# Part 2 of an attention and two-MoE kernel: four to three places for the split pairs, five to six for the output weights

## The chip, the cores and the metric

One core of a Trainium2 chip runs the whole program in one launch. The metric is the device time of one execution in microseconds; the median of the runs shown is quoted. TensorE (PE) has two clock levels, 1.2 and 2.4 GHz, and the profile gives the granted share of the higher one.

## The reference, cut to what matters

```python
attn = softmax(q @ mean8(k).T / sqrt(64)) @ mean8(v)      # 8 x 8 heads, 576 x 64
x = attn as 4608 tokens x 512
x = max(x @ w1, x @ w2, x @ w3) @ w_out                   # part 1's second half, d_ff 768
h = relu(x @ w_in)                                        # part 2: 512 -> 2048
out = (h * h) @ w_out2                                    # part 2: 2048 -> 512, float32
```

## The kernel before, in words

Part 1 (attention and the first MoE) runs in twelve blocks of 384 tokens and ends near 758 us. Part 2 runs in nine blocks `j` of 512 tokens. All products work on split numbers: a float32 value is written as a high half (ScalarE, L133) and a low half (the difference, VectorE, L134), and each product takes three matmuls (high by high, high by low, low by high). Both matrix products of part 2 are done by a seven-product scheme (Strassen's, in Winograd's form), which is why sums and differences of tiles (`add`, L644, and `minus`, L647) stand between them.

A block has four groups `gr`. Each group has an inner half and an outer half:

- `moe2_in` (L689): seven products with the resident weights `wi2s` (L673, 84 matmuls in all), gathered into the units `c0` to `c3` (one place each) and squared. The products use three PSUM banks `ps`; the first of a group is copied out by ScalarE at L707 into `c0`.
- `moe2_out` (L783): outer products in the order of `OUT`, four in groups 0 and 1, ten in groups 2 and 3 (called light and heavy below; 28 in a block, 252 in all). Each takes a fresh split pair `g` from the pool `g_p` (a pair of [128, 512] halves: 4 KB in each partition), one tile `wo2s` from the pool `wo_p` (also 4 KB), and does 12 matmuls into an accumulator (L797). The first eight of the 12 need only the high half of `g`, the last four need the low half.

The output weights don't stay on chip: `fetch_group` (L806) fetches each of the 252 tiles (512 KB) anew on SP's queue, once for each product. A fetch waits until the product that used its place has ended. Inner weights `wi2s` are fetched once, into `w3_p`, at the change from part 1 to part 2.

The program is not run in the order of the code: a planner with a simulated clock orders each engine's instructions before the launch, with the pools' places among its conditions. In the program before it has put matmuls of the next group's inner half between the outer products of a group; only three of the next group's products fit there, one a bank, until the copy at L707 frees the first. Each engine then runs its own list strictly in order.

At the border between blocks (`j`, group 3) VectorE and ScalarE also mix and split the next block's input: `load_y` (L607) fetches `yr` into places shared with the operands of groups 2 and 3, `mix_y` (L620) and `split_y` (L632) work on it.

Pools on the same side of the on-chip memory lie behind one another: `g_p`, `c_p`, `w3_p`, `wo_p`. With `reuse_waits="tile"` a tile waits only for the older tiles whose bytes it takes over; at the start of part 2 these are tiles of part 1.

Of the kernel before, what the change touches and what calls it, by code (L numbers as in the profile page):

```python
# [86 lines left out]
def leave(pool, size):  # L87

    pool.tile([P, size // 4], F32, name="unused", bufs=1)
# [3 lines left out]
def attention_moe_kernel(ctx: ExitStack, tc: tile.TileContext, q, k, v, vn, w1, w2, w3, wo1, wi2, wo2, out):  # L93
# [561 lines left out]
    add_moe1(NB1 - 1)  # L655
    run()
    s1.close()
    g_p = ctx.enter_context(tc.tile_pool(name="g_p", bufs=4, reuse_waits="tile"))
    c_p = ctx.enter_context(tc.tile_pool(name="c_p", bufs=1, reuse_waits="tile"))
    w3_p = ctx.enter_context(tc.tile_pool(name="w3_p", bufs=1, reuse_waits="tile"))  # L660
    wo_p = ctx.enter_context(tc.tile_pool(name="wo_p", bufs=5, reuse_waits="tile"))
    leave(w3_p, 160)
    leave(wo_p, 32)
    acc_ps = ctx.enter_context(tc.tile_pool(name="acc_ps", bufs=1, space=PSUM, reuse_waits="tile"))
# [208 lines left out]
```

## Time and profile before

| what | before |
|---|---|
| median of 3 runs | 1470.51 us (1463.79 to 1470.95) |
| the profiled execution | 1465.84 us, of it 1464.0 us span |
| PE busy | 1432.9 us, 98% of the span |
| DVE busy | 984.6 us, 67% |
| ACT busy | 763.9 us, 52% |
| DMA moved | 263.94 MB, mean 180 GB/s |
| fetches of output weights | 252 of 512 KB, median 5.7 us from issue to landing |
| chain that ended last | PE 88%, DMA 5%, ACT 3%, DVE 2% |

Times are of one execution on the chip. A bracket behind a row is the engine's idle time before it and what ended that. A matmul's end is modelled: it overlaps the next one, so the distance from one start to the next is less than the duration shown. Weight loads (PEld) overlap in the same way.

### The profile page before, as it was taken

How to read it: one execution, taken by the hardware profiler on the slowest of the kernel's cores; microseconds unless marked ns; L12 is line 12 of the kernel's file. 1: busy time of each engine (PE TensorE's matmuls, PEld its weight loads, DVE VectorE, ACT ScalarE, POOL GpSimd, SP SyncE). 2: the span in 40 equal slices, each digit the busy share in tenths (PEclk: the TensorE clock that was granted, in tenths of full speed). 3: DMA queues.
4: the chain of work that ended last, by engine and by line, in shares of the span. 5: the costliest groups of instructions: out<-in, count | busy, mean ns of one | idle time of the engine just before them, and what ended most of it. 6: DMA issues, size and time to landing. Idle time of an engine off the chain costs nothing.

```text
span 1464.0 us, 27554 instructions
## 1 busy us (share of the span) xinstructions
PE 1432.9 (98%) x10410; PEld 1409.8 (96%) x10410; DVE 984.6 (67%) x1778; ACT 763.9 (52%) x1983; POOL 182.2 (12%) x228
## 2 busy tenths in 40 slices
PE   6989999999999999999999999999999999999998
PEld 4879999999999999999999999999999999999998
DVE  5896466766765856656426768687776768686765
ACT  7794366655665646655314535353444445454443
POOL 3451012222222212222000000000000000000000
PEclk9899999999999999999999999999999999999999
DMA  7553135443355434422539856666666666565746
GB/s 225 185 168 110 53 115 173 141 134 123 120 164 176 126 124 130 130 101 79 187 116 370 290 196 212 220 210 224 229 231 225 227 216 214 198 245 174 274 144 229
DMA packets 118307, 263.94 MB, mean 180 GB/s; under 512 B 12672, under 2 KB 62848, under 8 KB 118176
## 3 DMA queue, kind: packets, MB, share of 16 engines
q1 hardware_dynamic: 111264, 252.75, 51.0%
q10 hardware_dynamic: 6912, 9.44, 1.8%
q8 instruction: 82, 1.34, 0.4%
q14 instruction: 49, 0.40, 0.1%
HBM read 213.91 MB, written 48.23 MB: 179 GB/s over the span
## 4 chain that ended last, share of the span: by engine, by line
PE 88%; DMA 5%; ACT 3%; DVE 2%; issue 1%; POOL 0%; SPq 0%; DVEq 0%; ACTq 0%; POOLq 0%
PE ps L513 28%; PE ps L673 23%; PE ps L532 10%; PE accB L797 6%; PE accA L797 6%; DMA wo2s<-wo_dram 4%; PE accF L797 3%; PE accE L797 3%; PE sc L353 2%; PE accD L797 2%; PE tr L381 2%; PE av L410 1%; PE av L409 1%; ACT ss L358 1%; DVE wbits L165 1%
## 5 line engine op out<-in xcount | busy, mean ns | idle before, releaser
L513 PE MATMUL ps<-x,w 128*128 128x384 f32 x2592 | 495.7, 342 | 3.3 <-ACT w L133 1.2
L513 PEld LDWEIGHTS ps<-x,w 128*128 128x128 f32 x2592 | 452.0, 190 | 6.1 <-ACT w L133 2.6
L673 PE MATMUL ps<-y,wi2s 128*128 128x256 f32 x3024 | 371.8, 277 | 0.5 <-DVE c L644 0.2
L673 PEld LDWEIGHTS ps<-y,wi2s 128*128 128x128 f32 x3024 | 356.6, 188 | 1.9 <-DVE c L644 0.8
L532 PE MATMUL ps<-h,wo 128*128 128x384 f32 x864 | 162.1, 339 | 3.2 <-POOL wo L134 2.4
L532 PEld LDWEIGHTS ps<-h,wo 128*128 128x128 f32 x864 | 149.5, 189 | 4.0 <-POOL wo L134 2.8
L686 ACT ACTIVATE c<-c 128x512 f32<-128x512 f32 x90 | 56.3, 627 | 167.2 <-DVE c L644 166.6
L644 DVE TENSOR_TENSOR c<-ps,c 128x512 f32<-128x512 f32 x144 | 98.2, 687 | 66.0 <-PE ps L673 64.5
L521 DVE TENSOR_TENSOR hm<-ps,hm 128x384 f32<-128x384 f32 x144 | 79.5, 552 | 72.3 <-PE ps L513 69.9
L133 ACT ACTIVATE g<-c 128x512 fp32r<-128x512 f32 x144 | 90.2, 626 | 56.7 <-DVE c L683 23.3
L797 PE MATMUL accA<-wo2s,g 128*128 128x256 f32 x864 | 115.8, 277 | 0.0
L797 PE MATMUL accB<-wo2s,g 128*128 128x256 f32 x864 | 110.9, 277 | 2.6 <-DMA wo2s<-wo_dram 1.9
L134 DVE TENSOR_TENSOR g<-c,g 128x512 fp32r<-128x512 f32 x144 | 97.6, 685 | 16.2 <-ACT g L133 16.2
L797 PEld LDWEIGHTS accA<-wo2s,g 128*128 128x128 f32 x864 | 107.1, 188 | 0.0
L358 ACT ACTIVATE ss<-sc,st 128x72 f32<-128x72 f32 (+1 forms) x320 | 97.9, 319 | 17.6 <-DVE st L355 15.4
L797 PEld LDWEIGHTS accB<-wo2s,g 128*128 128x128 f32 x864 | 103.9, 188 | 3.2 <-ACT o L766 1.6
L364 POOL TENSOR_TENSOR ss<-ss,st 128x432 f32<-128x432 f32 (+1 forms) x64 | 56.4, 882 | 265.7 <-DVE st L363 182.9
L413 DVE TENSOR_TENSOR xf<-av,xf 64x192 f32<-64x192 f32 (+1 forms) x112 | 50.7, 453 | 46.7 <-ACT xf L412 44.8
L385 DVE TENSOR_TENSOR pt<-tr,pt 72x192 fp32r<-72x192 f32 (+1 forms) x112 | 49.3, 449 | 41.4 <-ACT pt L384 40.1
L412 ACT ACTIVATE xf<-av 64x192 f32<-64x192 f32 (+1 forms) x112 | 45.4, 405 | 54.5 <-PE av L410 40.4
L133 ACT ACTIVATE h<-hm 128x384 fp32r<-128x384 f32 x72 | 37.7, 523 | 64.2 <-DVE hm L521 63.9
L358 ACT ACTIVATION_READ_ACCUMULATOR ss<-sc,st 128x1 f32 (+1 forms) x320 | 65.8, 206 | 0.0
(104 smaller groups left out, 1951.4 us busy)
## 6 DMA issues: line engine op xcount, KB each, us to landing
wo2s<-wo_dram SPq DMA_DIRECT2D x252, 512.0 KB, 5.7
wi2s<-wi_dram SPq DMA_DIRECT2D x24, 512.0 KB, 9.1
wraw<-in_wo_dram SPq DMA_DIRECT2D x22, 512.0 KB, 3.7
wraw<-in_w_dram SPq DMA_DIRECT2D x18, 512.0 KB, 3.4
y_dram<-ys ACTq DMA_DIRECT2D x48, 192.0 KB, 2.0
wraw<-in_wi_dram SPq DMA_DIRECT2D x16, 512.0 KB, 3.5
wi_dram<-wraw SPq DMA_DIRECT2D x16, 512.0 KB, 3.7
wo_dram<-wraw SPq DMA_DIRECT2D x64, 128.0 KB, 2.0
```

What stands on the lines that cost most here:

```text
L133: nc.scalar.activation(hi, src, AF.Copy)
L134: engine.tensor_tensor(out=lo, in0=src, in1=as_f32(hi), op=ALU.subtract)
L358: nc.scalar.activation(ss[:, i, h], src[:, i, h], AF.Exp, bias=st[:, 0, i, h : h + 1], accum_out=st[:, 1, i, h : h + 1],)
L364: nc.gpsimd.tensor_tensor(out=ss, in0=ss, in1=st[:, 2].rearrange("p g (h o) -> p g h o", o=1).to_broadcast([m, g, 2, SP]), op=ALU.mult,)
L413: nc.vector.tensor_tensor(out=xf[r], in0=av[r], in1=xf[r], op=ALU.add)
L513: nc.tensor.matmul(ps, lhsT=w1_t[f, e][:, a, kk * P : (kk + 1) * P], rhs=x[kk][:, c], start=(n == 0), stop=(n == 3 * KD - 1),)
L521: nc.vector.tensor_tensor(out=hm, in0=ps, in1=hm, op=ALU.max)
L532: nc.tensor.matmul(ps, lhsT=wo1_t[kk][:, a, d * P : (d + 1) * P], rhs=hs[kk][:, c], start=(n == 0), stop=(n == 3 * KF1 - 1),)
L644: nc.vector.tensor_tensor(out=out, in0=in0, in1=in1, op=ALU.add)
L673: nc.tensor.matmul(bank[:, u * HT : (u + 1) * HT], lhsT=wi2_t[2 * gr + u][i][:, a, o + kk * P : o + (kk + 1) * P], rhs=y_t[j][m][:, c, kk] ...
L686: nc.scalar.activation(c, c, AF.Relu)
L797: nc.tensor.matmul(bank[:, i * 256 : (i + 1) * 256], lhsT=g[:, a, u * HT + i * P : u * HT + (i + 1) * P], rhs=w[:, u, c], start=(n == 0 an ...
```

## The change

Two numbers of places change. Both tiles have 4 KB in each partition, so the pools' sum stays; `c_p` and `w3_p` and what lies in them move 4 KB down, and `wo_p` begins 4 KB lower.

```diff
-    g_p = ctx.enter_context(tc.tile_pool(name="g_p", bufs=4, reuse_waits="tile"))
+    g_p = ctx.enter_context(tc.tile_pool(name="g_p", bufs=3, reuse_waits="tile"))
     c_p = ctx.enter_context(tc.tile_pool(name="c_p", bufs=1, reuse_waits="tile"))
     w3_p = ctx.enter_context(tc.tile_pool(name="w3_p", bufs=1, reuse_waits="tile"))
-    wo_p = ctx.enter_context(tc.tile_pool(name="wo_p", bufs=5, reuse_waits="tile"))
+    wo_p = ctx.enter_context(tc.tile_pool(name="wo_p", bufs=6, reuse_waits="tile"))
```

## Rows read from the trace of the kernel before

**Rows 1.** Busy time by stretch: bounds, length, busy us (x instructions), clock, DMA share, GB/s.
```profile
758.00:1460.30 702.30, 696.75 (x6051) 692.82 (x6049) 504.70 (x799) 320.88 (x552) 0.00 (x0) 1.00 0.66 229
1460.30:1464.00 3.70, 0.00 (x0) 0.00 (x0) 0.61 (x1) 0.00 (x0) 0.00 (x0) 0.82 0.43 142
758.00:800.00 42.00, 41.53 (x352) 40.55 (x351) 25.95 (x40) 13.87 (x24) 0.00 (x0) 1.00 0.95 365
```

**Rows 2.** Waits of the weight loads from 758 us on: total, times, longest.
```profile
PEld accF L797 <- issue: 3.4, 8, 0.6
PEld accB L797 <- ACT o L766: 1.6, 1, 1.6
PEld accB L797 <- ACT qB L760: 0.9, 1, 0.9
PEld ps L673 <- DVE c L644: 0.8, 3, 0.4
PEld ps L673 <- DVE a L644: 0.7, 2, 0.4
PEld accB L797 <- issue: 0.6, 1, 0.6
PEld accE L797 <- issue: 0.5, 2, 0.3
```

**Rows 3.** PE's timeline, two of its waits for output weights: start, length, ..., [idle before].
```profile
994.50 1.61 PE L797 MATMUL accF<-wo2s,g 128*128 128x256 f32 x12 [0.39 <-DMA wo2s<-wo_dram]
...
1452.52 1.15 PE L797 MATMUL accB<-wo2s,g 128*128 128x256 f32 x8 [1.48 <-DMA wo2s<-wo_dram]
```

**Rows 4.** The chain of waits in order of time: start, length, what.
```profile
1011.19 2.72 PE accB L797 x24
...
1448.35 4.03 DMA wo2s<-wo_dram
```

**Rows 5.** The output weights' tiles over the whole program.
```profile
DMA to landing us min/median/max: 3.2/5.7/7.8
```

**Rows 6.** Busy time by stretch around two heavy groups, columns as before.
```profile
1112.00:1116.00 4.00, 4.00 (x38) 4.00 (x37) 4.00 (x8) 2.87 (x5) 0.00 (x0) 1.00 0.19 50
1116.00:1120.00 4.00, 4.00 (x38) 4.00 (x37) 4.00 (x7) 1.90 (x3) 0.00 (x0) 1.00 0.94 321
1120.00:1124.00 4.00, 4.00 (x37) 4.00 (x37) 1.56 (x3) 1.64 (x3) 0.00 (x0) 1.00 0.98 329
...
1136.00:1140.00 4.00, 4.00 (x38) 4.00 (x37) 4.00 (x8) 4.00 (x9) 0.00 (x0) 1.00 0.01 2
...
1152.00:1156.00 4.00, 4.00 (x38) 4.00 (x37) 2.67 (x4) 0.00 (x0) 0.00 (x0) 1.00 1.03 409
```

**Rows 7.** ACT's waits from 640 us on: total, times, longest.
```profile
ACT g L133 <- PE accD L797: 28.2, 27, 2.8
...
ACT g L133 <- PE accA L797: 22.1, 19, 3.9
```

**Rows 8.** ACT's timeline at the end of a group 3: the last pairs, then L707.
```profile
1146.63 0.63 ACT L133 ACTIVATE g<-a 128x512 fp32r<-128x512 f32 x1 [0.84 <-PE accD L797]
1147.99 0.63 ACT L133 ACTIVATE g<-c 128x512 fp32r<-128x512 f32 x1 [0.73 <-DVE g L134]
1149.38 0.60 ACT L707 ACTIVATE c<-ps 128x512 f32<-128x512 f32 x1 [0.76 <-DVE g L134]
```

**Rows 9.** DVE's timeline in the same group.
```profile
1128.51 0.69 DVE L647 TENSOR_TENSOR t<-yr 128x512 f32<-128x512 f32 x1 [2.09 <-DMA yr<-y_dram]
...
1147.29 0.69 DVE L134 TENSOR_TENSOR g<-a,g 128x512 fp32r<-128x512 f32 x1
1147.99 0.69 DVE L644 TENSOR_TENSOR qA<-accD,qA 128x512 f32<-128x512 f32 x1
1148.65 0.69 DVE L134 TENSOR_TENSOR g<-c,g 128x512 fp32r<-128x512 f32 x1
```

**Rows 10.** PE's timeline in the same group.
```profile
1150.51 1.53 PE L797 MATMUL accE<-wo2s,g 128*128 128x256 f32 x12
1151.87 1.43 PE L673 MATMUL ps<-y,wi2s 128*128 128x256 f32 x11
1153.14 1.53 PE L797 MATMUL accF<-wo2s,g 128*128 128x256 f32 x12
```

**Rows 11.** SP's timeline at the change from part 1 to part 2.
```profile
761.56 1.85 SPq L601 DMA_DIRECT2D wo2s<-wo_dram  x4
763.46 22.61 SPq L596 DMA_DIRECT2D wi2s<-wi_dram  x19
```

## The prediction, made before the changed kernel ran

> **What bounds the kernel now.** I read the page first: PE is busy for 98% of the span, and part 2 is the tighter half. Then the busy time by stretch: from 758 us to the last matmul PE is busy in 696.75 of 702.30 us at full granted clock, and 3.7 us follow without any PE work [rows 1]. So the change can only remove what PE still waits for in 702 us, or add to it. The number of matmuls stays.
>
> Those waits come from the third view, the waits of the weight loads [rows 2]. I take the loads and not the matmuls, since a matmul's modelled end hides a short pause: 24 matmuls take 2.72 us in the chain [rows 4], 0.113 us each, against 0.277 us shown for one. A load is shown with 0.188 us, so each wait in its list is still 0.075 us too short. Waits labelled "issue" at the accumulators F, B and E are 3.4, 0.6 and 0.5 us in 8, 1 and 2 cases; PE's own timeline names their cause in the larger ones, a tile of output weights that has not landed [rows 3]. The wait of 1.6 us at accB belongs to them too: the list gives it to ACT, but the matmul behind it starts at 1452.52, the moment the fetch that started at 1448.35 is in (4.03 us) [rows 3, 4]. Together 6.1 us in 12 waits, plus 12 x 0.075 = 7.0 us. Everything else PE waits for here is 0.9 + 0.8 + 0.7 us in six waits [rows 2].
>
> Why the tiles are late: a fetch takes its place from an earlier product. With five places, the fetch for product n+5 starts when product n ends, and products n+1 to n+4 cover it. A product is 12 matmuls, 1.36 us; four cover 5.44 us. The median fetch takes 5.7 us, the longest 7.8 [rows 5]. The planner fills the difference with matmuls of the next group, which is why the waits are small and why they occur in 11 of the heavy groups' products and once at the very end, where no next group is left.
>
> **The change part by part.**
>
> *Sixth place for the weights (gain).* Cover rises to five products, 6.8 us, above the median landing. Also, at the start of a heavy group one more of its ten tiles is already there, and it was fetched in a stretch with idle DMA engines (share 0.19 and 0.01 ahead of the two groups shown, against 0.94 to 1.03 inside them [rows 6]). A fetch starts up to 1.36 us earlier; each of the eleven waits inside part 2 is at most 0.6 + 0.075 us, so I count them all as gone: 4.5 + 0.8 = 5.3 us. The one at the end (1.6 + 0.1) shrinks by what an earlier start brings, at most 1.36 us; I take 1.2. Gain 6.5 us; bounds 0 (below, under the rivals) and 7.0. Of these bounds I am near the upper one, because the waits have rows and the shift is longer than each of them.
>
> *Third instead of fourth place for the pairs (cost).* The high half of pair n+3 now waits for the end of product n, in place of pair n+4. ACT already meets this wait: 28.2 us in 27 waits and 22.1 us in 19 behind accD and accA [rows 7], and PE does not suffer. The loop is: product ends, ACT is told (0.2 us, an estimate), high half 0.63 us, low half 0.69 us (1146.63 to 1147.98 [rows 8, 9]), about 1.55 us in all; two other products (2.72 us) run meanwhile, where three (4.08 us) do now. So 1.17 us are left, and another 0.9 us for the low half, which only the last four of the 12 matmuls read. In the group shown, the pair of the ninth product is complete at 1147.98 and used at 1150.51 [rows 9, 10]; with its place freed one product later it would be complete near 1149.4. Queued behind a waiting ACT are the copy L707 and the squares; behind the waiting low half on DVE are the sums out of PSUM. The group's last pair would move from 1147.99 to about 1149.4, and L707 behind it from 1149.38 to about 1150.8 [rows 8]; its bank is then free at 1151.4, and PE opens the next product there at 1151.87 [rows 10]. So this is covered too, but by 0.5 us only.
>
> Where the cover is thinnest is the border between blocks: DVE has next to no pause from 1128.51, when `yr` lands, to 1147.29 [rows 6, 9]. There are eight borders. I charge 0.2 us each, 1.6 us. Bounds: 0, by the cover just shown; and 18 heavy groups x 1.36 us = 24.5 us, if each lost one whole product. I am near the lower bound since each row followed leaves some cover.
>
> *Move by 4 KB.* `c_p` and `w3_p` take over other tiles of part 1. The four first output tiles are issued at 761.56 and the last inner weights after 763.46 [rows 11]; the DMA engines are 0.95 busy to 800 us while PE loses under 0.5 us of 42 [rows 1]. A start some 2 us earlier or later changes what stands in the queue, not PE's work. 0, bounds -0.5 and +2 us.
>
> *A new plan.* The planner sees other conditions and may order part 2 otherwise. PE's work is the same in any order; what can go or come are waits of the kind of the other 2.4 us. 0, bounds -2.4 and +2.4 us.
>
> Sum: 1465.84 - 6.5 + 1.6 = 1460.9 us for an execution like the profiled one (span 1464.0 and 1.8 around it). The median of the runs shown is 0.32% above that execution; on it I forecast 1460.9 x 1470.51 / 1465.84 = 1466 us (rounded up from 1465.6), 0.3% less than before.
>
> **Rivals.**
>
> *R1, the pairs become the loop (slower).* If two DVE instructions of 0.69 us stand between a high half and its low half (as the sum into qA does once at 1147.99 [rows 9]), the loop takes 1.55 + 1.37 = 2.92 us, over the 2.72 of two products: 0.2 us lost on each of the seven pairs that wait, and at the group's end L707 comes 1.36 + 1.37 = 2.7 us later, 0.8 us more than the 1.9 us from its end at 1149.98 to 1151.87. That is 2.2 us a group. It decides where DVE has no pause, in the eight groups 3 at a border: 17.6 us, less 6.5 gained: 11.1 us slower, near 1482 us. For it: the full DVE there. Against: three pairs are still made ahead of their products, and the planner knows the place count and can put the sums elsewhere.
>
> *R2, the DMA engines are the limit (no change).* In a heavy group ten tiles and, at a border, the next input of 1 MB pass: 5.24 + 1.05 MB. At the 365 GB/s of the fullest long stretch [rows 1] that is 17.2 us; PE spends 13.6 us on ten products and at most 4.1 on the 36 matmuls (three products of the next group) that fit between. With all engines at 0.94 and more [rows 6] an earlier issue only lengthens the queue. Then the waits stay or move, and the pairs cost 1.6 us: 1470 to 1472 us. Against: the extra tile comes out of the idle stretch ahead, and the waits are under 0.7 us, less than one tile's 1.4 us at that rate.
> The Trainium skill bears on R2: "DMA: Bandwidth & Descriptors", section Specifications, gives about 358 GB/s as the limit of HBM for a core. By it, an estimate of 17.6 us for the same bytes, the supply would bind a little more, and the time would be that of R2. The trace shows 409 GB/s in one stretch of 4 us [rows 6] and 365 over 42 us [rows 1], above that figure, so I hold R2 as less likely than the rule makes it.
>
> *R3, the plan gets better beyond the waits.* With tiles early the planner also has no reason to break off products, and the other 2.4 us go as well, with no cost at the pairs: 1465.84 - 7.0 - 2.4 = 1456.4, on the median's scale 1461 us. For it only that these waits exist [rows 2]; they are behind DVE and ACT, which the change doesn't relieve.
>
> That the change doesn't do what it says I leave out: both numbers are plain place counts, and SP's fetches are held by places.
>
> **How the numbers follow.** A measurement of this kernel can hardly tell less than 0.5% (7.4 us) from no change; faster means below 1463.2, slower above 1477.9. Forecast: chance 0.58, 1466 us, its own range 1462 to 1471. R1: 0.20. R2: 0.14. R3: 0.08. Faster: R3 mostly (0.06) and the lower edge of the forecast (0.09), 0.15. Slower: R1 but for its mild cases (0.17), and 0.02 from the costs of move and plan, 0.19. Same: 0.66. The range must take in R3 and most of R1: 1459 to 1480 us.
>
> **What would show it.** Right: the waits "issue" at accF, accB and accE under 1.5 us in all, the fetch median unchanged or up to 1 us longer (six in flight), ACT's waits for `g` behind the accumulators clearly above the two rows' 50 us, PE busy within 1 us of its share. Step for the pairs wrong: PE or its loads wait for DVE or ACT at L134 or L133 in groups 2 and 3, or L673 waits for L707. R2: the waits for output weights stay while landings grow to 7 us and more. The prediction fails if the span changes by more than 8 us either way, or if part 1 changes by as much as part 2.

## The result, and the profile after

| | before | after |
|---|---|---|
| median of 6 runs | 1470.09 us | 1480.08 us (1477.43 to 1482.42) |
| the profiled execution | 1465.84 us, span 1464.0 | 1477.43 us, span 1475.6 |

The changed kernel takes 1.008 times as long (95% interval 1.0057 to 1.0103). One execution of before, 4052.96 us, is no guide to anything and the ratio leaves it out. I forecast 0.3% less; it became 0.8% more, 0.08 us past the upper end of my range. The waits below are those of one execution of each kernel, and the one of before lies 4.3 us under its median.

The loss is in part 2. Busy time by stretch of the changed kernel, from its first matmul of part 2 to its last, columns as in [rows 1]:

```profile
755.60:1471.40 715.80, 702.95 (x6050) 695.87 (x6048) 501.95 (x798) 321.71 (x552) 0.00 (x0) 1.00 0.64 225
```

702.3 us became 715.8, at full granted clock in both. Part 1 has the same lists of instructions (on ACT all but four of 1478) and took 2.6 us less in this execution, so the span grew by 11.6 only.

What the weight loads waited for in part 2 of the changed kernel (total, times, longest), to be set against [rows 2]:

```profile
PEld ps L673 <- DVE c L644: 11.9, 19, 1.0
PEld accF L797 <- ACT g L133: 3.0, 6, 0.6
PEld ps L673 <- ACT c L687: 2.9, 7, 0.4
PEld accB L797 <- ACT qB L760: 0.9, 1, 0.9
PEld ps L673 <- DVE a L644: 0.7, 2, 0.4
```

The waits at the accumulators fell from 6.1 us in 12 cases to 3.0 in 6 (the label says ACT; the matmuls' own list puts 1.9 us in 5 of them down to output weights). In their place stands a new one: the inner half's products (L673) wait 11.9 + 2.9 us for a free PSUM bank, in 26 cases against 0.8 us in 3 before. With 0.075 us more for each wait, as in the prediction: 14.8 + 2.0 - 0.8 - 0.2 = 15.8 us more there, 3.5 less at the accumulators, 12.3 of the 13.5 us.

The waits for the banks come in seven clusters, one at each border between blocks but the first: at the end of group 2 and in the inner half of group 3. One of them, first in the weight loads' timeline of the changed kernel:

```profile
1136.78 1.46 PEld L673 LDWEIGHTS ps<-y,wi2s 128*128 128x128 f32 x12 [0.16 <-DVE c L644]
1138.58 1.45 PEld L673 LDWEIGHTS ps<-y,wi2s 128*128 128x128 f32 x12 [0.35 <-DVE c L644]
1140.44 1.48 PEld L673 LDWEIGHTS ps<-y,wi2s 128*128 128x128 f32 x12 [0.42 <-ACT c L687]
...
1143.98 1.12 PEld L673 LDWEIGHTS ps<-y,wi2s 128*128 128x128 f32 x9 [0.96 <-DVE c L644]
```

then DVE at the same place:

```profile
1128.17 0.69 DVE L134 TENSOR_TENSOR g<-a,g 128x512 fp32r<-128x512 f32 x1 [0.67 <-ACT g L133]
1129.54 0.69 DVE L134 TENSOR_TENSOR g<-c,g 128x512 fp32r<-128x512 f32 x1 [0.68 <-ACT g L133]
1130.90 0.69 DVE L644 TENSOR_TENSOR c<-ps,c 128x512 f32<-128x512 f32 x1 [0.66 <-ACT c L707]
1135.43 0.69 DVE L647 TENSOR_TENSOR t<-yr 128x512 f32<-128x512 f32 x1 [3.84 <-DMA yr<-y_dram]
1136.04 0.68 DVE L644 TENSOR_TENSOR c<-ps,c 128x512 f32<-128x512 f32 x1
1136.64 0.68 DVE L134 TENSOR_TENSOR y<-yr,y 128x512 fp32r<-128x512 f32 x1
```

and the end of the group on PE and the loads of `yr` on SP:

```profile
1131.65 1.53 PE L797 MATMUL accF<-wo2s,g 128*128 128x256 f32 x12
1133.02 7.21 PE L673 MATMUL ps<-y,wi2s 128*128 128x256 f32 x56
```
```profile
1126.62 2.57 SPq L601 DMA_DIRECT2D wo2s<-wo_dram  x3
1129.28 1.85 SPq L616 DMA_DIRECT2D yr<-y_dram  x4
```

Read from the bottom: the group's last outer product ends at 1133.0, the last four loads of the next block's input `yr` are issued from 1129.28 to 1131.1, the last lands near 1135.4. DVE stands 3.84 us before `t<-yr`, and the sum out of PSUM that is next in its list waits behind it. That sum is ready at about 1133.9: it needs 36 of the inner half's 84 matmuls, 28 are done when the group ends (56 follow), and eight more take 0.9 us. From `t<-yr` on DVE has no pause. Each further sum has two other instructions ahead of it, so the sums start 1.80 us apart (1136.04, 1137.84 and so on), while PE needs one for each product of 1.36 us; so PE is held at bank after bank and not only once. In [rows 9] the same instruction waits for the same load, 2.09 us, and starts at 1128.51, but there the group's last product ends only at 1128.8 and the next sum is not ready before 1129.7. Over the borders `t<-yr` starts 0.3 to 2.0 us before the group's last product ends in the kernel before, and 1.7 to 3.3 us after it in the changed one.

### The profile page after: what moved, and what is told of

It is laid out like the page before. It is cut to its first block, busy times and chain, and to the rows that moved or that the text cites. A ratio compares the mean times of both kernels' runs of the same rounds, so it can differ in the third digit from the quotient of the medians.

```text
span 1475.6 us, 27639 instructions
## 1 busy us (share of the span) xinstructions
PE 1437.3 (97%) x10410; PEld 1412.4 (96%) x10410; DVE 979.6 (66%) x1778; ACT 764.5 (52%) x1983; POOL 181.1 (12%) x228
## 4 chain that ended last, share of the span: by engine, by line
PE 84%; DMA 6%; DVE 5%; ACT 3%; issue 2%; SPq 1%; POOL 0%; DVEq 0%; ACTq 0%; POOLq 0%
PE ps L513 28%; PE ps L673 20%; PE ps L532 10%; PE accA L797 6%; PE accB L797 6%; PE accE L797 3%; PE accF L797 3%; DMA wo2s<-wo_dram 3%; PE accD L797 2%; PE sc L353 2%; PE tr L381 2%; DVE c L644 1%; ACT ss L358 1%; PE av L410 1%; DMA yr<-y_dram 1%
## 5 line engine op out<-in xcount | busy, mean ns | idle before, releaser
L673 PE MATMUL ps<-y,wi2s 128*128 128x256 f32 x3024 | 377.8, 278 | 10.1 <-DVE c L644 9.2
L673 PEld LDWEIGHTS ps<-y,wi2s 128*128 128x128 f32 x3024 | 358.9, 188 | 15.9 <-DVE c L644 11.9
L133 ACT ACTIVATE g<-c 128x512 fp32r<-128x512 f32 x144 | 89.4, 627 | 98.8 <-PE accB L797 41.7
L644 DVE TENSOR_TENSOR c<-ps,c 128x512 f32<-128x512 f32 x144 | 98.3, 688 | 58.8 <-PE ps L673 51.0
L134 DVE TENSOR_TENSOR g<-c,g 128x512 fp32r<-128x512 f32 x144 | 98.1, 687 | 40.9 <-ACT g L133 40.9
L133 ACT ACTIVATE h<-hm 128x384 fp32r<-128x384 f32 x72 | 37.7, 523 | 64.4 <-DVE hm L521 63.9
```

Of the source, the lines that this page charges most:

```text
L133: nc.scalar.activation(hi, src, AF.Copy)
L134: engine.tensor_tensor(out=lo, in0=src, in1=as_f32(hi), op=ALU.subtract)
L644: nc.vector.tensor_tensor(out=out, in0=in0, in1=in1, op=ALU.add)
L673: nc.tensor.matmul(bank[:, u * HT : (u + 1) * HT], lhsT=wi2_t[2 * gr + u][i][:, a, o + kk * P : o + (kk + 1) * P], rhs=y_t[j][m][:, c, kk] ...
```

## The experiments

All ratios are to the kernel before, run on the same chip beside them; its median there was 1469.49 us for the first four experiments and 1469.99 us for the last four.

**One half of the change alone.**
```diff
 after, with
-    wo_p bufs=6
+    wo_p bufs=5
```


> Three places for the pairs, five for the weights: one half of the change alone (4 KB stay unused). Theory A (the missing pair place makes the last pairs of group 2 late, so the places that the next block's input yr shares come free late, yr lands after the group's last product, and DVE, in order, holds the sums out of PSUM behind it): the border waits of L673 for DVE are there as in the changed kernel (8 to 12 us), and the waits for output weights of the kernel before are partly back: 1480 to 1488 us. Theory B (the sixth weight place moves fetches ahead of yr on SP's queue): no border loss, 1468 to 1473 us. Theory C (any changed condition gives another plan, with losses by chance): anything, with DVE's list unlike that of the changed kernel.

Measured 1492.43 us, ratio 1.0143 (1.0116 to 1.0171). DVE's list is nearly that of the changed kernel: by line, operation and tiles, 11 of its 1778 instructions stand elsewhere, against 113 when it is compared with the kernel before. The weight loads wait

```profile
PEld ps L673 <- DVE c L644: 12.1, 20, 1.5
PEld accB L797 <- ACT g L133: 10.1, 7, 1.9
PEld accF L797 <- issue: 2.9, 9, 0.6
```

The border loss is all there, so it comes from the pairs' place and not from the weights'. It is 4 us beyond my range, and the waits at the accumulators did not come back at their old 6.1 us but at two and a half times that (15.4 us without `qB`'s).

**Four places and six.**
```diff
 after, with
-    g_p bufs=3
+    g_p bufs=4
 and, for the space, wi2_t[7] = wi2_t[6] in place of a fetch
```


> Four places for the pairs and six for the weights; to have the 4 KB, the inner weights of the last pair of 128-row strips are left out and those of the pair before are used in their stead (4 of 28 fetches at the change from part 1, the same matmuls). Theory A: no border loss and the waits for weights shorter: 1462 to 1467 us. Theory B: the border loss of the changed kernel, 1477 to 1483 us.

Measured 1463.67 us, ratio 0.9955 (0.9938 to 0.9973). The sixth weight place alone gives about the gain that I had forecast for it (5.8 us by the medians). The four fetches that are left out can hardly be part of it: in the stretch where they run PE loses under 0.5 us of 42 [rows 1]. Theory B falls here, since there is no border loss of that size:

```profile
PEld ps L673 <- DVE c L644: 2.4, 7, 0.7
```

But `yr` is late here as well. `t<-yr` starts 0.5 to 2.1 us after the group's end at all eight borders:

```profile
1127.78 0.69 DVE L647 TENSOR_TENSOR t<-yr 128x512 f32<-128x512 f32 x1 [5.38 <-DMA yr<-y_dram]
1125.85 4.03 PE L673 MATMUL ps<-y,wi2s 128*128 128x256 f32 x34
```

One thing that differs is how far PE is when the group ends. Only 14 of the 84 inner matmuls are done there (34 more follow before the first wait), against 28 in the changed kernel, so PE comes to each bank 14 matmuls, 1.6 us, later after the group's end. How late `yr` may land hangs on that too, and not on the group's end alone.

**The last place of `yr` freed earlier.** In group 2, `OUT` becomes (4,1) (2,0) (5,1) (2,1) (6,1) **(5,0)** (6,0) (4,0) (3,1) (3,0); the place counts stay three and six.


> The changed kernel with one product moved: in group 2 the product (5,0), whose operand holds the last shared place of yr, comes three products earlier; group 3 keeps its order. Theory A: the place comes free some 4 us earlier, yr lands before the group's last product, the border waits of L673 for DVE fall under 3 us in all: 1463 to 1470 us. Theory B: fetches still stand ahead of yr, 1477 to 1482 us.

Measured 1457.61 us, ratio 0.9918 (0.9903 to 0.9932): 5.4 us under my range, and faster than both kernels. DVE at the border shown above, and the loads' waits:

```profile
1122.57 0.69 DVE L647 TENSOR_TENSOR t<-yr 128x512 f32<-128x512 f32 x1 [1.97 <-DMA yr<-y_dram]
```
```profile
PEld accF L800 <- ACT g L133: 1.2, 2, 1.0
PEld accB L800 <- ACT qB L763: 0.9, 1, 0.9
PEld ps L673 <- DVE a L644: 0.7, 2, 0.4
PEld ps L673 <- ACT c L707: 0.4, 2, 0.2
PEld ps L673 <- DVE c L644: 0.3, 1, 0.3
```

The group's last product ends at 1126.1 there, 3.5 us after `t<-yr` has started.

**`yr` on another queue.**
```diff
-    nc.sync.dma_start(out=yr[:, i, t : t + n], ...)
+    nc.gpsimd.dma_start(out=yr[:, i, t : t + n], ...)
```


> The changed kernel with the loads of yr on GpSimd's queue, which has no other work in part 2, in place of SP's. Theory A: the places come free as late as before, so yr lands at most 1 us earlier: 1475 to 1481 us. Theory B: yr no longer stands behind fetches that wait for PE, the border loss goes: 1463 to 1469 us.

Measured 1467.45 us, ratio 0.9991 (0.9975 to 1.0006). Neither theory had this right. GpSimd's own list shows that the loads came no earlier; with nothing else on the queue they wait for the split pair:

```profile
1126.21 2.11 POOL L616 DMA_DIRECT2D yr<-y_dram  x4 [2.90 <-DVE g L134]
```

Counted from the end of the group's last product (1130.1 here), the last load is issued 2.3 us ahead, as in the changed kernel. What is new is DVE's list: the planner has put the first four sums of the inner half ahead of the work on `yr`.

```profile
1127.96 0.69 DVE L644 TENSOR_TENSOR c<-ps,c 128x512 f32<-128x512 f32 x1 [0.67 <-ACT c L707]
1131.19 0.69 DVE L644 TENSOR_TENSOR c<-ps,c 128x512 f32<-128x512 f32 x1 [2.54 <-PE ps L673]
1132.55 0.69 DVE L644 TENSOR_TENSOR c<-ps,c 128x512 f32<-128x512 f32 x1 [0.67 <-PE ps L673]
...
1136.99 0.68 DVE L647 TENSOR_TENSOR t<-yr 128x512 f32<-128x512 f32 x1
```

So a late landing by itself makes no product wait for a bank (0.3 us in one wait for DVE's sums here); PE waits 5.3 us for pairs at accA and accB instead. Theory A was made narrower for the next runs: the loss needs both, a late `yr` and a list that has `yr` ahead of the sums.

**The order of DVE's list, with SP's list unchanged.** Before `mix_y`, one element of `t5` and one of the low half of `y1` are written from the sum of the sixth product:
```diff
+    nc.vector.tensor_copy(t5[:1, 0, :1], c[:1, :1])
+    nc.vector.tensor_copy(y1[:1, 1, 0, :1], c[:1, :1])
```


> The changed kernel, yr loaded as there, but the first two DVE instructions on yr (into t5 and into the low half of y1) are held behind the sum of the sixth product of group 3 by a one-element DVE write each. Theory A, made narrower (yr lands late since its place comes free late, and the loss arises because DVE's list has the work on yr ahead of the sums out of PSUM): yr lands as late as in the changed kernel, the sums are no longer behind it, the border waits of L673 for DVE fall from 11.9 to under 4 us: 1464 to 1470 us. Theory D (DVE has too much work at the border in any order): 1475 to 1482 us.

Measured 1467.15 us, ratio 0.998 (0.9963 to 0.9996). The last load of `yr` is again issued 1.9 to 3.3 us before the group's end (6.5 at the first border), against 1.4 to 3.3 (6.3) in the changed kernel, and the waits for DVE's sums are gone:

```profile
PEld accA L811 <- ACT g L133: 4.0, 10, 0.6
PEld accB L811 <- ACT g L133: 1.9, 2, 1.3
...
PEld ps L685 <- DVE c L656: 0.3, 1, 0.3
```

SP's list is the same as in the changed kernel, instruction for instruction. PE's and ACT's are not: the planner orders every run anew, and 535 of 10410 matmuls and 67 of 1983 instructions of ACT stand elsewhere. Theory D falls: in another order DVE frees the banks in time. Not all is won back: the split of the next pairs now meets the held work, 5.9 us at accA and accB, and the kernel is 9.5 us behind the one with the early product.

**The early product without the change.** The new order of group 2 in the kernel before (four and five places).


> The kernel before (four pair places, five weight places) with the product (5,0) of group 2 three products earlier. Theory A: there is next to no border loss to remove there (0.6 us) and the waits for output weights stay: 1466 to 1471 us. Theory E (the moved product is a better order of itself, whatever the places): 1456 to 1462 us.

Measured 1465.27 us, ratio 0.9975 (0.9962 to 0.9987), 0.7 us under my range: a gain of its own of 4.7 us by the medians, far from the 22.5 us that it is worth at three and six (1480.08 to 1457.61).

**Own places for `yr`.** `yr` of blocks 1 to 8 in tiles of `c_p` (and the leave-out of the second experiment).


> The changed kernel with own places for yr in blocks 1 to 8, so that its loads wait for no split pair; to have the 8 KB, the inner weights of the last pair of strips are left out and those of the pair before are used (the same matmuls). Theory A: yr is there before the group's end, border loss under 3 us: 1459 to 1467 us. Theory D: 1475 to 1482 us.

Measured 1457.48 us, ratio 0.9921 (0.9902 to 0.9941), 1.5 us under my range. With three pair places and no wait of `yr` for a pair, the sums' wait for DVE is 0.3 us:

```profile
PEld accB L800 <- ACT qB L763: 0.9, 1, 0.9
...
PEld ps L676 <- DVE c L647: 0.3, 1, 0.3
```

This run changes both conditions at once: the loads of `yr` are issued about a block ahead of their border, and `t<-yr` runs that much ahead too. It shows that the loss hangs on `yr`'s place, and does not tell the two conditions apart.

**Three and five with the early product.**


> Three pair places, five weight places, and the product (5,0) of group 2 three products earlier. Theory A: no border loss, but the waits for output weights of the kernel with three and five (15 us against 6 before) stay: 1468 to 1476 us; so the sixth weight place is worth 11 to 18 us where pairs have three places. If those waits came from the border loss, 1458 to 1464 us.

Measured 1467.2 us, ratio 0.9983 (0.9968 to 0.9998), 0.8 us under the range. The waits at the accumulators are 8.3 us in all without `qB`'s, near the 6.1 of the kernel before and not 15 us; the largest:

```profile
PEld accF L800 <- issue: 3.7, 9, 0.8
PEld accB L800 <- ACT g L133: 1.8, 2, 0.9
PEld accF L800 <- ACT c L707: 1.1, 2, 0.6
```

So the large waits for weights of the first experiment went away with the border loss, and my reading of them as a price of three pair places with five weight places was wrong. How a border makes later weights late was not traced.

The three runs with the early product (three and six, four and five, three and five places) give the terms free of the border loss, by the medians: the sixth weight place 1467.2 to 1457.6, 9.6 us gained; the fourth pair place 1467.2 to 1465.3, 1.9 us, which is not clear of noise, since the intervals of the two ratios overlap.

## Why the prediction was wrong

*What bounds the kernel, and the gain.* Right. The gain is there as counted: 5.8 us by the second experiment, 9.6 by the last comparison, against the 6.5 of the sum. In the changed kernel itself only 3.5 us show; I had expected the accumulators' waits under 1.5 us, which holds only where the border loss is gone (1.2 us at accF in the third experiment). One row was passed over: PE's loads also wait 0.4 us in two cases behind L707, in both kernels alike. The landing times did not grow, 5.2 us at the median against 5.7 [rows 5], and the sixth place alone brought 1463.67 us and not the 1470 to 1472 of R2. So R2 falls; its own sum did not bind either, with 17.2 us of supply against 13.6 + 4.1 = 17.7 us of PE. The limit of about 358 GB/s that the Trainium skill gives ("DMA: Bandwidth & Descriptors", section Specifications) pointed to R2's time too; the changed kernel's trace has 371 GB/s from 758 to 800 us, above it.

*The third place for the pairs, inside a group.* Right in its path. ACT's waits for `g` behind all the accumulators went from 57.1 us (50.3 of them in [rows 7]) to 102.7:

```profile
ACT g L133 <- PE accA L797: 42.5, 36, 4.2
ACT g L133 <- PE accB L797: 41.7, 26, 2.3
...
ACT g L133 <- PE accD L797: 16.4, 19, 3.3
```

and PE hardly felt it: without the border loss the place costs 1.9 us, not clear of noise, where I had put nothing inside a group.

*The step that failed* is the border: "I charge 0.2 us each, 1.6 us." It measured 15.8 us in seven borders, 2.3 each. I had followed a later pair to PE, to L707 and to the squares. I had not asked who else waits for the split: it also reads the last place that `yr` shares, so the load on SP waits for it. SP's own list has that wait, here of the changed kernel:

```profile
SPq L616 <- DVE g L134: 62.3, 15, 8.0
```

The kernel before has it too, with 59.6 us in 16 cases, so it was there to be read. I had read in [rows 9] that DVE waits 2.09 us for `yr` and taken it as the start of a full stretch. It was the end of a chain from the pair's place to the load to `t<-yr`, and in DVE's order the sums that free PE's banks stand behind that. The cover was about one microsecond between the landing of `yr` and the next sum; the change moved the split of (5,0) from 7.0 to 4.2 us before the group's end at the border shown, and the cover was used up. My signs of a wrong step looked at L133, L134 and L707; the loss showed at L644, which none of them named.

*R1* gave nearly the right time (1482 us) and the right engine by luck, with a wrong mechanism: no pair's loop came to limit PE between the outer products, L707 is not what PE waits for, and the loss lies ahead of group 3's outer products, not at their end. *R3* asked for the other waits to go as well; they stayed.

*A new plan.* I set it at 0, bounds 2.4 us. Both kernels' lists have `t<-yr` ahead of the same sum, so the plan did not become worse in kind; it lacked the slack for a load that comes late. Why the planner puts `yr` first on SP's queue and last on GpSimd's was not tried; that it reckons with an earlier landing on SP's is only argued. The last 1.2 us of part 2's growth lie in pauses too short for the list and were not followed up.

## What to carry to other kernels

Before taking a place from a pool, list every reader that will end later, and for each the places that it frees; follow those to the queue that refills them, not only to the engine that is the bound. A wait on a DMA in an in-order engine's list is a debt of everything behind it: look at what stands behind, and how long it could wait before the bound engine does. A mixed change is worth taking apart: here one half gained and the other lost more, and moving one product kept the gain and removed the loss.

## What the runs showed of the hardware

A sixth place for the output weights did not lengthen the median fetch. From issue to landing the 512 KB tiles took 4.7 to 5.6 us at the median in the six kernels with six places (5.2 in the changed one), and 5.5 to 5.7 us in the four with five. The longest rose, from 7.4 to 7.8 us with five places to 9.0 to 9.8 us with six.

DVE kept to its list's order: at the border shown it stood 3.84 us for a load, while the sum behind that had been ready for about 1.5 us.
